# Unit 0's second token group with seven block products, unit 1's v in unit 0's buffer, and the sums of w2 behind the conversions

## The chip, the cores and the metric

One core of one Trainium2 chip runs the program. The metric is the device time of one execution in microseconds (us); the kernel before takes 663.11 us, the median of three runs that lie between 662.74 and 663.75. The engines have these names in the profile: PE is TensorE (matrix products), PEld its weight loads, DVE is VectorE, ACT is ScalarE, POOL is GpSimd and SP is SyncE. DMA queues are fed from POOL, SP and ACT.

## The reference

A gated linear recurrence with complex decay runs over 768 steps for 4 x 8 heads of width 48; its outputs, laid out as 3072 tokens of 384 numbers, go through a two-layer network with a squared relu.

```python
mag = np.sqrt(a_re * a_re + a_im * a_im)
scale = np.minimum(mag, 0.999) / (mag + 1e-06)
a_re_n, a_im_n = (a_re * scale, a_im * scale)
for t in range(S):
    new_re = ar * S_re - ai * S_im
    new_im = ar * S_im + ai * S_re
    S_re, S_im = (new_re + kv, new_im)              # kv: outer product of k and v at t
    y[:, :, t] = np.einsum('bhd,bhde->bhe', q[:, :, t], S_re)
h = x @ w_in                                         # x: y as (3072, 384); w_in (384, 2048)
r = np.maximum(h, 0.0)
out = (r * r) @ w_out                                # w_out (2048, 384)
```

## The kernel before

The 3072 tokens are taken in six **units** of 512. For each unit the program does two kinds of work.

The **chain** of a unit runs mostly on DVE and ACT. It normalises the decays (L982 to L1006), multiplies them up within groups of four steps (`inner`, L1026 and L1034), turns the group products to the other layout on PE (L1060), scans them (L1107 to L1188), turns them back (L1060 again), and then, in `apply`, forms the scaled keys and queries: four products (L1261), two sums (L1278, into `aq`), squares on ACT (L1292), their sum (L1299), a logarithm and an exponential on ACT (L1301, L1306), and the keys and queries (L1309 to L1326, into `f`). The table `HOMES` may put the two sums (and the sum of squares) of one `apply` on PE, as products with the identity into a PSUM bank (L1267, L1268); the squares are then two ACT operations (L1286), and later steps read the bank.

The **pairs** of a unit (four, of two heads each) are the attention proper: keys and queries are transposed, either on PE (`turn_pe`, L1440, copied out by ACT at L1444; the table `BY_PE` names these pairs) or by DVE's transpose and DMAs (`turn`, L1414, L1419); scores on PE (L1461), masked by DVE into `A` (L1464); products of keys and v for the carried state (L1489, summed by DVE at L1503); outputs (L1520 and L1524, the "mix"), copied by ACT (L1533) and put into `xT` by DMA. Scores and mixes use parts of the PE array, all other products the whole array.

The **two-layer network** of a unit comes in two token groups of 256. The first layer is L1571 (96 matmuls for a unit, squared relu on ACT at L1604 and L1605). The second layer is either `dense` (32 matmuls with 384 columns for a group, L1619, copied by ACT at L1624) or `seven` (the groups in the table `SEVEN`, and both of the last unit): seven block products instead of eight, as 56 matmuls with 192 columns (L1682), with eight DVE sums of the hidden values (`put`, L1698), and DVE sums of the results (L1707) in place of ACT copies. `seven` needs four sums of blocks of w2, made once by `sums_of_w2` as eight DVE operations (L1672) into the tile `T`.

The weights arrive as 8-byte floats in 16 pieces, eight of w_in and eight of w_out, and are **converted** by ACT (L859) and DVE (L866, then L870, then L873). Pieces with an index of at least `SOON` use a second ACT operation (L864) in place of L870.

L1380 are products with the identity whose results nobody reads; the planner puts them into PE's gaps of the first 60 us.

The rows of a profile name a matmul of 4-byte numbers twice (its two passes): 32 matmuls L1619 are 64 records. Transposes on PE are recorded once.

The order on each engine is not written by hand. Every step is given to a planner (`Plan`) with an engine, an assumed duration, what it reads and writes, and a rank; `Plan.order` fills a modelled schedule greedily by rank, and the program is emitted in that order. `LANES`, `LANDED`, `SETTLED`, `GROUP`, `MLAT` and such are numbers of that model: for instance, after the modelled time `SETTLED` PE puts scores and mixes next to each other where it can. `ROOM` is the number of units that have a v buffer (and spare buffers inside `T`) of their own: with `ROOM = 2` unit 1 keeps its v, a third `QT` and a third `A` in the tile `T`, and the sums of w2, which need that space, come after unit 1's pairs.

Of the kernel before, what the change touches and what calls it, by code (L numbers as in the profile page):

```python
# [481 lines left out]
class Plan:  # L482
# [3 lines left out]
    MARGIN = 0.3  # L486
    SLACK = 1.7
    RATE = 280e3
    LANES, LANDED = 8, 0.2
    STOP, COLD = 2.4, 3.5  # L490
    TURN = 0.12
    SETTLED, GROUP = 90.0, 6
    HOLD, URGENT, FILL = {"DVE": 0.15, "ACT": 0.8}, (2, 0.2), (2, 0.2)
    DRAIN = {"DVE": 0.12, "ACT": 0.13}

# [127 lines left out]
def fast_path(ctx, tc, q, k, v, a_re, a_im, moe_w_in, moe_w_out, out, flag):  # L623
# [10 lines left out]
    NP = H // 2  # L634
# [13 lines left out]
    Y = HH * W * D  # L648
    EARLY = 2
    FINE = [(0, 0), (0, 1), (1, 0), (1, 1), (2, 0), (2, 1)]  # L650
    SOON = 4
    LEAD = 2
    LATER = 6
    HOMES = {(0, 0, 0): ("sc0", "sc1", None), (0, 0, 1): ("yp", "tr1", "tr0")}
    FILLS = 16, 12, 8
    LOADS = 1.0, 4.0
    NEAR, GLAT, TLAT, MLAT = 7.5, 2.0, 1.0, 1.0
    BY_PE = [(0, i) for i in range(NP)] + [(1, i) for i in range(3)]
    ROOM = 2
    SEVEN = [(1, 0), (1, 1), (2, 0), (2, 1), (3, 0), (3, 1), (4, 0), (4, 1), (5, 0), (5, 1)]  # L660

    dve, pool, act, sp = nc.vector, nc.gpsimd, nc.scalar, nc.sync
    pe = nc.tensor
# [89 lines left out]
    def vs(n):  # L753
        return n % 2 if n < ROOM else 0

    def tt(n):
        return n / 960.0 + 0.07
# [34 lines left out]
    CHAIN, PAIR, DENSE, CONV, LATE = 2, 1, 3, 3, 5  # L792
# [54 lines left out]
    def convert(i):  # L847
        held = tuple(plan.wrote[("a", 1)][1]) if SOON <= i < NPIECE else ()
        _, t, keys, dst, n, wk = piece(i)
# [4 lines left out]
        def part(dtype, i):  # L854
# [5 lines left out]
             after=later)  # L860
        mixed = SOON <= i < 2 * NPIECE
        if mixed:
# [90 lines left out]
    def chain(n):  # L953
# [284 lines left out]
        def apply(z, p, np):  # L1238
# [12 lines left out]
            rk = late[z]  # L1251
            home = HOMES.get((n, z, p), (None, None, None))
            held = [[(b,)] if b else [] for b in home]
# [117 lines left out]
    def take(kind, n):  # L1371
        s = slot[kind]
        slot[kind] = s + 1
        return s % n
# [9 lines left out]
    def pairs(n, which):  # L1384
# [9 lines left out]
        def turn(i):  # L1394
            z = i // 2
            s = take("QT", 3 if 0 < n < ROOM else 2)
            t = QT[s].rearrange("p (i x) -> p i x", i=W)
# [26 lines left out]
        def turn_pe(i):  # L1424
            z = i // 2
            s = take("QT", 3 if 0 < n < ROOM else 2)
            got["T", i] = s
# [20 lines left out]
        def score(i, h):  # L1448
# [3 lines left out]
            sa = bank[b].rearrange("p (j t) -> p j t", j=W)  # L1452
            a = take("A", 3 if 0 < n < ROOM else 2)
            got["A", i, h] = a
# [99 lines left out]
        for i in which:  # L1554
            (turn_pe if (n, i) in BY_PE else turn)(i)
            for h in range(2):
# [6 lines left out]
    def dense(n, grp):  # L1563
# [11 lines left out]
        spare = ["sc0", "sc1", "yp"] if n < EARLY and grp == 0 else []  # L1575
        joint = (n, grp) in SEVEN
        fs = [(j, j + NT) if joint else (2 * j, 2 * j + 1) for j in range(NT)]
# [82 lines left out]
    def sums_of_w2():  # L1660
        for h in range(2):
            fl, fu = slice(4 * h, 4 * h + 4), slice(NT + 4 * h, NT + 4 * h + 4)
            b00, b01 = w2[:, fl, 0:DH], w2[:, fl, DH:DM]
            b10, b11 = w2[:, fu, 0:DH], w2[:, fu, DH:DM]
            t3, t2, t4, s2 = (TW[r][:, fl] for r in range(4))
            lo, up = parts_of(h, 0), parts_of(h, 1)
            for o, x0, x1, reads, writes in (
                    (t3, b11, b01, lo + up, 0), (s2, b01, b00, lo, 3),
                    (t2, b11, s2, up + [("T", 3, h)], 1), (t4, b10, t2, up + [("T", 1, h)], 2)):
                writes = [("T", writes, h), ("t", writes)] + (tkeys[writes] if writes < 3 else [])  # L1670
                step("DVE", tt(4 * DH), reads, writes, lambda o=o, x0=x0, x1=x1:
                     dve.tensor_tensor(out=o, in0=x0, in1=x1, op=ALU.subtract),  # L1672
                     (PAIR, 1.5))

    def gk(x, r, h):
        return [("gh"[x], HW * h + i, r) for i in range(HW)]
# [219 lines left out]
    for n in range(NU):  # L1896
        load(n)
        if n == 0:
            for i in range(NPIECE):
                fetch(i)  # L1900
            for i in range(SOON):
                convert(i)
        rest = chain(n)
        if n == 0:
            for j in (0, 1, 2):
                fetch(NPIECE + j)
        if n == 0:
            fill(FILLS[2], [("lv", 0)], lv[:, 0])
            for z in range(2):
                rest(z)  # L1910
                pairs(n, (2 * z, 2 * z + 1))
            for i in range(SOON, NPIECE):
                convert(i)
        else:
            rest(0, 1)
            pairs(n, range(NP))
        if n == ROOM - 1:
            sums_of_w2()
        if n == 0:
            step("POOL", 0.2, xk(0, [NM - 1]), [("gate", 2)], lambda: pool.tensor_copy(  # L1920
                out=gate[:, 2:3], in_=xT[:, 0, NM - 1, L - 1:L]), (CONV, 0))
            for j in (3, 4):
                fetch(NPIECE + j, False)
            for j in range(NPIECE):
                convert(NPIECE + j)
                if j < 3:
                    fetch(NPIECE + 5 + j, False)
        if n == NU - 1:
            eleven(n)
        for grp in range(2):  # L1930
            (seven if n == NU - 1 else dense)(n, grp)
    for i in range(2 * NPIECE):
# [58 lines left out]
```

## Time and profile before

| what | value |
| --- | --- |
| median of three runs | 663.11 us (662.74 to 663.75) |
| the profiled execution | 663.12 us |
| its span, first to last instruction | 661.2 us |
| PE busy | 620.8 us, 94% |
| DVE busy | 583.9 us, 88% |
| ACT busy | 347.0 us, 52% |
| mean granted TensorE clock | 0.99 |
| start of the first long run of first-layer products (L1571), unit 0 | 83.44 us |
| start of the same for unit 1, 2, 3, 4 | 191.19, 288.35, 386.43, 483.24 us |
| start of the last unit's first layer (L1827) | 580.75 us |

The profiled execution is one of the runs that agree with the median within 0.01 us. Read it by stages: up to about 60 us PE has little to do and DVE is busy; from there PE works without a break to the end, unit by unit, some 97 us each, and fills the time in which the next unit's chain runs on DVE with the network of the unit before.

### The profile page before, as it was taken

What the parts mean: (1) busy time and instruction counts of PE and PEld (TensorE: products, weight loads), DVE (VectorE), ACT (ScalarE), POOL (GpSimd) and SP (SyncE); (2) the same over time, 40 slices, a digit from 0 to 9 for tenths busy, and PEclk for the clock granted to TensorE, in tenths of its full rate; (3) what the DMA queues carried; (4) which work ended last, traced back from release to release, by engine and by line L of the source; (5) the groups of instructions that cost most, each with busy time, mean ns of one, the idle gap of its engine ahead of it and who ended that gap; (6) DMA issues with size and microseconds to landing.
All of it is one profiled execution on the core that took longest, in us unless ns stands there. A gap on an engine that the chain in (4) does not pass through costs nothing.

```text
span 661.2 us, 12107 instructions
## 1 busy us (share of the span) xinstructions
PE 620.8 (94%) x4454; PEld 555.5 (84%) x4454; DVE 583.9 (88%) x1191; ACT 347.0 (52%) x606; POOL 118.7 (18%) x198
## 2 busy tenths in 40 slices
PE   0378999999999999999999999999999999999996
PEld 0357887687779988999989989989999989988996
DVE  7999999898998999998989888998879989559971
ACT  7748979985746345348263357363366352045300
POOL 7401040401100032040121040111040111032200
PEclk9979999999999999999999999999999999999999
DMA  7953686305530055570056571046470054367730
GB/s 227 313 224 79 150 208 187 70 3 153 143 89 1 7 133 143 134 185 1 12 128 165 133 159 30 14 117 169 121 181 0 25 121 89 92 202 262 250 113 27
DMA packets 55268, 80.35 MB, mean 122 GB/s; under 512 B 11392, under 2 KB 37920, under 8 KB 55200
## 3 DMA queue, kind: packets, MB, share of 16 engines
q0 software_dynamic: 15424, 42.12, 22.5%
q1 hardware_dynamic: 35168, 31.93, 19.0%
q10 hardware_dynamic: 4608, 5.44, 3.2%
q8 instruction: 37, 0.61, 0.4%
q14 instruction: 31, 0.25, 0.1%
HBM read 48.76 MB, written 4.72 MB: 81 GB/s over the span
## 4 chain that ended last, share of the span: by engine, by line
PE 89%; DVE 7%; ACT 2%; issue 1%; DMA 1%; SPq 0%; DVEq 0%; ACTq 0%
PE d L1571 29%; PE d L1682 28%; PE d L1619 6%; PE sc L1461 5%; PE tr L1489 4%; PE yp L1520 3%; PE yp L1524 2%; PE d L1827 2%; PE tr L1827 2%; PE sc L1571 2%; PE sc L1827 1%; PE tr L1060 1%; DVE f L1261 1%; PE d L1440 1%; PE tr L1440 1%; PE yp L1571 1%
## 5 line engine op out<-in xcount | busy, mean ns | idle before, releaser
L1571 PE MATMUL d<-xT,w 128*128 128x256 f32 x888 | 198.5, 380 | 0.0
L1571 PEld LDWEIGHTS d<-xT,w 128*128 128x128 f32 x888 | 166.9, 190 | 23.1 <-issue 0.6
L1682 PE MATMUL d<-T,g 128*128 128x192 f32 x576 | 98.7, 327 | 0.0
L1682 PEld LDWEIGHTS d<-T,g 128*128 128x128 f32 x576 | 93.6, 190 | 0.3
L1604 ACT ACTIVATE g<-d 128x512 f32<-128x512 f32 x74 | 44.1, 596 | 83.6 <-PE d L1571 68.3
L1682 PE MATMUL d<-w,g 128*128 128x192 f32 x432 | 76.1, 329 | 0.0
L1637 POOL DMA_DIRECT2D out_dram<-ot x40 | 25.6, 644 | 277.6 <-DVE ot L1707 223.3
L1682 PEld LDWEIGHTS d<-w,g 128*128 128x128 f32 x432 | 70.4, 190 | 1.6 <-issue 0.7
L1362 POOL DMA_DIRECT2D KC<-f x60 | 32.4, 558 | 141.1 <-DVE f L1326 99.1
L1698 DVE TENSOR_TENSOR g<-g 128x512 f32<-128x512 f32 x72 | 48.5, 689 | 8.7 <-ACT g L1605 4.5
L1605 ACT ACTIVATE g<-g 128x512 f32<-128x512 f32 x80 | 50.5, 631 | 2.6
L1261 DVE TENSOR_TENSOR f<-aq,xn 128x384 f32<-128x384 f32 (+1 forms) x72 | 46.8, 687 | 0.0
L1619 PE MATMUL d<-w,g 128*128 128x384 f32 x128 | 44.0, 490 | 0.0
L1414 DVE STREAM_TRANSPOSE aq<-f 128x384 f32<-128x384 f32 (+1 forms) x51 | 42.7, 912 | 0.2
L1026 DVE TENSOR_TENSOR f<-aq 128x384 f32<-128x384 f32 x72 | 37.2, 554 | 0.8
L1461 PEld LDWEIGHTS sc<-QT 96*64 96x64 f32 x736 | 33.5, 137 | 3.6 <-issue 2.8
L1461 PE MATMUL sc<-QT 96*64 96x128 f32 (+1 forms) x736 | 36.0, 249 | 0.2 <-ACT QT L1444 0.2
L1619 PEld LDWEIGHTS d<-w,g 128*128 128x128 f32 x128 | 23.5, 190 | 13.7 <-issue 0.2
L1707 DVE TENSOR_TENSOR ot<-ot,d 128x192 f32<-128x192 f32 x70 | 23.7, 350 | 12.5 <-PE d L1682 12.0
L1464 DVE TENSOR_TENSOR A<-sc,mask 128x512 f32<-128x512 f32 x45 | 29.9, 685 | 3.2 <-PE sc L1461 3.1
L1533 ACT COPY yt<-yp 112x512 f32<-112x512 f32 (+1 forms) x20 | 11.6, 579 | 37.2 <-PE yp L1524 37.1
L1292 ACT ACTIVATE f<-aq 128x768 f32<-128x768 f32 (+1 forms) x16 | 17.3, 1082 | 24.7 <-DVE aq L1278 24.6
(279 smaller groups left out, 1119.5 us busy)
## 6 DMA issues: line engine op xcount, KB each, us to landing
QT<-aq SPq DMA_DIRECT2D x136, 64.0 KB, 2.0
f<-in_moe_w_in_dram POOLq DMA_DIRECT2D x8, 768.0 KB, 6.9
f<-in_moe_w_out_dram POOLq DMA_DIRECT2D x8, 768.0 KB, 5.1
QT<-aq ACTq DMA_DIRECT2D x68, 64.0 KB, 2.1
KC<-f POOLq DMA_DIRECT2D x40, 96.0 KB, 3.4
out_dram<-ot POOLq DMA_DIRECT2D x40, 96.0 KB, 3.7
xT<-yt SPq DMA_DIRECT2D x34, 96.0 KB, 2.4
T<-in_moe_w_out_dram POOLq DMA_DIRECT2D x4, 768.0 KB, 9.9
```

The source lines that it names most:

```text
L1026: lambda c=c, j=j: dve.tensor_tensor(out=f[:, j], in0=a[:, :, :, c - 1], in1=a[:, j, :, c].unsqueeze(1).to_broadcast([C, 2, HH, D]), op=AL ...
L1261: lambda j=j, r=r: dve.tensor_tensor(out=f4[:, j, r], in0=a[:, r], in1=over(j), op=ALU.mult), rk)
L1362: lambda i=i, p0=p0, m=m, src=src, queue=queue: queue.dma_start(out=kc[p0:p0 + m, i], in_=src),
L1414: lambda src=src, dst=dst: dve.transpose(out=dst, in_=src), rank)
L1461: pe.matmul(sa[p0:p0 + CH, j, t0:], lhsT=T[:, j, 1, h, t0:t0 + CH], rhs=T[:, j, 0, h, t0:], start=True, stop=True)
L1571: pe.matmul(ps, lhsT=w1[:, f // FP, m, ts(f % FP, C)], rhs=xT[:, n % 2, m, ts(grp, G)], start=(m == 0), stop=(m == NM - 1))
L1604: act.activation(out=o, in_=ps, func=AF.Relu)
L1605: act.activation(out=o, in_=o, func=AF.Square)
L1619: pe.matmul(ps, lhsT=gt[:, f % 2, ts(i, C)], rhs=w2[:, f], start=(f == 0), stop=(f == NF - 1))
L1682: pe.matmul(bank[b][:, 0:DH], lhsT=gsets[x][h][:, j - HW * h, r], rhs=w(j), start=first and j == 0, stop=last and j == NT - 1)
L1698: lambda: dve.tensor_tensor(out=g[:, :, o], in0=g[:, :, x0], in1=g[:, :, x1], op=op),
L1827: pe.matmul(ps[:, jj], lhsT=u[:, ts(jj, C)], rhs=v_, start=i == 0, stop=i == len(terms) - 1)
```

## The change

Tables and numbers of the planner change, one step's rank, and the place of one call.

```diff
-    LANES, LANDED = 8, 0.2
+    LANES, LANDED = 7, 0.2
-    SETTLED, GROUP = 90.0, 6
+    SETTLED, GROUP = 200.0, 6
...
-    SOON = 4
+    SOON = 3
-    HOMES = {(0, 0, 0): ("sc0", "sc1", None), (0, 0, 1): ("yp", "tr1", "tr0")}
+    HOMES = {(0, 0, 1): (None, None, "tr0")}
-    NEAR, GLAT, TLAT, MLAT = 7.5, 2.0, 1.0, 1.0
-    BY_PE = [(0, i) for i in range(NP)] + [(1, i) for i in range(3)]
-    ROOM = 2
-    SEVEN = [(1, 0), (1, 1), (2, 0), (2, 1), (3, 0), (3, 1), (4, 0), (4, 1), (5, 0), (5, 1)]
+    NEAR, GLAT, TLAT, MLAT = 7.5, 2.0, 1.0, 1.2
+    BY_PE = [(0, i) for i in range(NP)] + [(1, i) for i in range(4)]
+    ROOM = 1
+    SEVEN = [(0, 1), (1, 0), (1, 1), (2, 0), (2, 1), (3, 0), (3, 1), (4, 0), (4, 1), (5, 0), (5, 1)]
...
                 step("DVE", tt(4 * DH), reads, writes, lambda o=o, x0=x0, x1=x1:
                      dve.tensor_tensor(out=o, in0=x0, in1=x1, op=ALU.subtract),
-                     (PAIR, 1.5))
+                     (CHAIN, 1.05))
...
             pairs(n, range(NP))
-        if n == ROOM - 1:
-            sums_of_w2()
         if n == 0:
...
         if n == NU - 1:
             eleven(n)
+        if n == ROOM - 1:
+            sums_of_w2()
```

Counted over the whole program, the order has on PE 32 matmuls L1619 fewer (64 to 32), 56 matmuls L1682 more (560 to 616), 16 transposes L1440 more (112 to 128), and 4 each of L1267 and L1268 fewer (5 to 1 each). On DVE there are 4 more L1278 (32 to 36), 8 more L1698 (80 to 88), 7 more L1707 (70 to 77), 3 fewer L1414 (51 to 48) and 1 fewer L870 (4 to 3). On ACT there is one more L864 and 4 more L1444, two fewer L1624 and one more L1702, and four L1286 have become two more L1292. Unit 1's pairs now change on PE between parts of the array and the whole array 24 times, before 16 times.

The first place is DVE at the end of unit 0's pairs. `A` and `St` belong to the last pair from the second mask row on; `w_66` is w_in under conversion; L982 is the first step of unit 1's chain. Before:

```order
L870 SCALAR_TENSOR_TENSOR w_66<-g,w_66 128x768
L873 ISA w_66<-g,w_66 128x1536
L866 TENSOR_SCALAR w_66<-w_67 128x768
L870 SCALAR_TENSOR_TENSOR w_66<-w_67,w_66 128x768
L1464 TENSOR_TENSOR A_87<-sc_114,mask 128x512
L1464 TENSOR_TENSOR A_88<-sc_115,mask 128x512
L982 TENSOR_TENSOR f_70<-f_70 128x768
L1503 TENSOR_TENSOR St_90<-tr_117,St_90 96x96 x2
```

With the change:

```order
L982 TENSOR_TENSOR f_70<-f_70 128x768
L1503 TENSOR_TENSOR St_89<-tr_116,St_89 96x96 x2
L873 ISA w_66<-g,w_66 128x1536
L1503 TENSOR_TENSOR S_86<-tr_117,St_89 96x96
L866 TENSOR_SCALAR w_66<-g 128x768
L870 SCALAR_TENSOR_TENSOR w_66<-g,w_66 128x768
L873 ISA w_66<-g,w_66 128x1536
L1464 TENSOR_TENSOR A_87<-sc_114,mask 128x512
L1464 TENSOR_TENSOR A_88<-sc_115,mask 128x512
L866 TENSOR_SCALAR w_66<-w_67 128x768
L1503 TENSOR_TENSOR St_90<-tr_117,St_90 96x96 x2
```

L982 has moved ahead of the last pair's masks; one L870 is gone, and the L866 that stood before it has moved behind the masks.

The second place is DVE where unit 1's scan begins (L1087 and L1107, which read the turned products); `w_67` is w2, and `T` and `T_73` its sums. Before:

```order
L866 TENSOR_SCALAR w_67<-T 128x768
L1026 TENSOR_TENSOR f_71<-aq_69 128x384
L1034 TENSOR_TENSOR xn<-f_71 128x192 x2
L873 ISA w_67<-T,w_67 128x1536
L1087 COPY e<-ce 128x3
L1089 MEMSET e 128x3
L1087 COPY e<-ce 128x3
L1089 MEMSET e 128x3
L1107 TENSOR_TENSOR KC_76<-e 128x384
```

With the change:

```order
L1672 TENSOR_TENSOR T<-w_67 128x768
L873 ISA w_67<-T,w_67 128x1536
L1034 TENSOR_TENSOR xn<-f_71 128x192 x2
L1672 TENSOR_TENSOR T<-w_67,T_73 128x768
L1672 TENSOR_TENSOR T<-w_67 128x768
L1672 TENSOR_TENSOR T<-w_67,T 128x768
L1087 COPY e<-ce 128x3
L1089 MEMSET e 128x3
L1087 COPY e<-ce 128x3
L1089 MEMSET e 128x3
L1672 TENSOR_TENSOR T<-w_67,T_73 128x768
L1107 TENSOR_TENSOR KC_76<-e 128x384
```

Four of the sums of w2 stand in the L1672 rows before L1087, a fifth just before and a sixth just after L1107; before, one of these six stood in unit 1's pairs and five behind them. The other two (`T_73`) stand among the conversions in both.

The third place is PE at unit 1's scan; L1060 turns the scanned products (`xn`) back, between products of unit 0's first layer (L1571) for the second token group. Before:

```order
L1619 MATMUL d_112<-w_67,g 128x384 x4
L1571 MATMUL d_111<-xT,w_66 128x256 x6
L1571 MATMUL d_112<-xT,w_66 128x256 x6
L1571 MATMUL d_113<-xT,w_66 128x256 x3
L1060 MATMUL tr_116<-ident,xn 128x128 x3
L1571 MATMUL d_113<-xT,w_66 128x256 x3
L1060 MATMUL tr_117<-ident,xn 128x128 x3
L1571 MATMUL d_111<-xT,w_66 128x256 x6
L1571 MATMUL d_112<-xT,w_66 128x256 x6
L1571 MATMUL d_113<-xT,w_66 128x256 x6
L1571 MATMUL d_111<-xT,w_66 128x256 x6
L1619 MATMUL d_112<-w_67,g 128x384 x4
```

With the change:

```order
L1619 MATMUL d_112<-w_67,g 128x384 x4
L1571 MATMUL d_113<-xT,w_66 128x256 x3
L1571 MATMUL d_111<-xT,w_66 128x256 x6
L1571 MATMUL d_112<-xT,w_66 128x256 x6
L1571 MATMUL d_113<-xT,w_66 128x256 x6
L1571 MATMUL d_111<-xT,w_66 128x256 x3
L1060 MATMUL tr_116<-ident,xn 128x128 x3
L1060 MATMUL tr_117<-ident,xn 128x128 x3
L1571 MATMUL d_111<-xT,w_66 128x256 x3
L1571 MATMUL d_112<-xT,w_66 128x256 x6
L1571 MATMUL d_113<-xT,w_66 128x256 x6
L1571 MATMUL d_111<-xT,w_66 128x256 x6
L1682 MATMUL d_112<-w_67,g 128x192 x4
```

Before, 15 of the L1571 shown stand ahead of the first L1060 `ident` and three between the two; with the change 24 stand ahead of the first and none between, and behind them come L1682 in place of L1619. Counted from the program's start, 69 L1571 stand ahead of the first before and 75 with the change, and 32 L1619 in both.

## The prediction, made before the change was run

> **What bounds the kernel now.** I read the engines' totals and the chain of waits first, then windows by stage, then PE's waits.
>
> ```profile
> PE 620.8 (94%) x4454; PEld 555.5 (84%) x4454; DVE 583.9 (88%) x1191; ACT 347.0 (52%) x606; POOL 118.7 (18%) x198
> PE 89%; DVE 7%; ACT 2%; issue 1%; DMA 1%; SPq 0%; DVEq 0%; ACTq 0%
> ```
>
> PE has the largest total and 89% of the chain. But the totals mix stages, so the windows come next (span, then busy time of PE, PEld, DVE, ACT, POOL, granted clock, DMA share, GB/s):
>
> ```profile
> 30.00:40.00 10.00, 3.15 (x15) 3.18 (x16) 9.06 (x36) 6.34 (x11) 2.90 (x4) 0.51 1.02 318
> 60.00:83.00 23.00, 22.54 (x304) 20.11 (x304) 22.31 (x47) 20.28 (x32) 3.01 (x6) 1.00 0.63 147
> 83.00:151.00 68.00, 67.78 (x292) 52.10 (x289) 65.61 (x141) 57.67 (x95) 16.68 (x24) 1.00 0.45 118
> 151.00:191.00 40.00, 40.00 (x388) 30.75 (x386) 36.91 (x68) 24.74 (x48) 5.95 (x10) 1.00 0.52 143
> ```
>
> Up to 60 us DVE is full and PE mostly waits. From 60 to 151 both are full: PE 22.54 of 23 and 67.78 of 68, DVE 22.31 and 65.61. After 151 PE has no gap, while DVE has 3 us in 40. The waits of PE (total, times, longest) say where DVE holds it:
>
> ```profile
> PE d L1380 <- DVE yt L1119: 8.4, 1, 8.4
> PE d L1440 <- DVE f L1326: 2.3, 2, 1.6
> PE tr L1060 <- DVE xn L1188: 0.7, 2, 0.5
> PE tr L1520 <- DVE St L1503: 0.5, 1, 0.5
> ```
>
> Three places count for this change: the first keys of unit 0 (L1440 on L1326), the last sum of its pairs (L1520 on L1503), and the scan of unit 1, where PE waits for L1188:
>
> ```profile
> 134.14 0.55 PE L1060 MATMUL tr<-ident,xn 128*128 128x128 f32 x3 [0.22 <-DVE xn L1188]
> ```
>
> There DVE arrives 0.22 us after PE, so any work that DVE gains before this point arrives at PE almost undiminished. Everything behind it is PE work without a gap. So the end moves by how much later PE gets past unit 1's scan, plus the change of PE work behind it, plus new waits. Units 2 to 5 keep their order but for a few runs of products that are split otherwise.
>
> **Term 1: DVE's work up to unit 1's scan.** What matters on DVE is how its queue is composed between the end of unit 0's scan and L1188.
>
> ```profile
> 49.30 1.02 DVE L1278 TENSOR_TENSOR aq<-f 128x384 f32<-128x384 f32 x2
> 78.30 0.55 DVE L866 TENSOR_SCALAR w<-w 128x768 uint32<-128x768 uint32 x1
> 78.89 0.96 DVE L870 SCALAR_TENSOR_TENSOR w<-w,w 128x768 uint32<-128x768 uint32 x1
> 79.77 1.28 DVE L1464 TENSOR_TENSOR A<-sc,mask 128x512 f32<-128x512 f32 x2
> 80.97 0.95 DVE L982 TENSOR_TENSOR f<-f 128x768 f32<-128x768 f32 x1
> 81.83 0.53 DVE L1503 TENSOR_TENSOR St<-tr,St 96x96 f32<-96x96 f32 x2
> ```
>
> Rows overlap slightly; from start to start an L1278 takes 0.47 (two in 0.94), L870 0.88 (78.89 to 79.77) and L982 0.86 (80.97 to 81.83). Four L1278 come back from PE: +1.88. One conversion loses its L870: -0.88. L982 and the L866 pass the masks in opposite directions and are ahead of the last sum of the state in both orders: 0. So that sum comes 1.0 us later. The sums moved into the scan weigh more:
>
> ```profile
> 118.75 0.96 DVE L873 CUSTOM_DVE_ANT_0 w<-T,w 128x1536 uint16<-128x1536 uint16 x1 [0.17 <-ACT T L864]
> 121.68 0.96 DVE L873 CUSTOM_DVE_ANT_0 w<-T,w 128x1536 uint16<-128x1536 uint16 x1 [0.37 <-ACT T L864]
> 123.22 0.60 DVE L1087 COPY e<-ce 128x3 f32<-128x3 f32 x1 [0.27 <-ACT e L1075]
> 133.27 1.49 DVE L1188 TENSOR_TENSOR xn<-KC 128x384 f32<-128x384 f32 x2
> 193.54 2.88 DVE L1672 TENSOR_TENSOR T<-w,T 128x768 f32<-128x768 f32 x3
> ```
>
> Three L1672 take 2.88, about 0.9 each from start to start; six of the eight now stand ahead of the first L1188 instead of in or behind unit 1's pairs: +5.3. They fill DVE's waits for ACT, 0.17, 0.37 and 0.27: -0.8. L1188 thus comes 1.0 + 5.3 - 0.8 = 5.5 us later. The order of PE gives part of this back: 75 L1571 stand ahead of the first L1060 `ident` in place of 69, and 21 instead of 24 stand behind the second. Their price:
>
> ```profile
> 88.02 5.18 PE d L1571 x24
> 136.15 10.53 PE L1571 MATMUL d<-xT,w 128*128 128x256 f32 x48
> ```
>
> A matmul is two records, so 0.216 x 2 = 0.43 us. The second L1060 needs the second of the two L1188, which ends at 133.27 + 1.49 = 134.76 before and 5.5 later, at 140.3, now. PE then needs 0.4 for its three transposes, so it goes on at 140.7, against 136.15 before: +4.5. Three matmuls fewer are left behind it: -1.3. That makes +3.2; I take **+3.0**, as the added work may use small gaps of DVE. Does PE really get there too early? It is itself delayed by the last sum (1.0), by two L1571 that it did ahead of that sum and now does behind it (four records, 0.86), and by the six extra ones (12 records, 2.6):
>
> ```profile
> 79.64 1.10 PE L1571 MATMUL d<-xT,w 128*128 128x256 f32 x4
> ```
>
> That is 4.5 against DVE's 5.5, so PE waits about 1 more than the 0.22. The bounds: if L1188 does not hold PE, only its own 1.3 to 1.9 is left (1.3 where the L866 that now stands behind the masks takes less than the L982 that stood there); if DVE's waits for ACT stay, +3.8 to +4.0.
>
> **Term 2: PE's work behind it.** The second group of unit 0 swaps 32 L1619 (64 records) for 56 L1682 (112 records); 16 L1440 are added, as unit 1's last pair is turned on PE.
>
> ```profile
> 103.56 5.16 PE d L1619 x16
> 211.97 5.20 PE d L1682 x32
> 73.88 1.77 PE d L1440 x16
> ```
>
> 64 x 5.16/16 = 20.6 goes; 112 x 5.20/32 = 18.2 and 16 x 1.77/16 = 1.8 come: **-0.7**. So the eighth of the second layer that is saved, 2.4 us, is mostly spent on the turned pair. The three L1414 that the pair needed are gone from DVE, 2.4 us by the row below, in a stretch where PE sets the pace: 0.
>
> ```profile
> 169.34 2.47 DVE L1414 STREAM_TRANSPOSE aq<-f 128x768 f32<-128x768 f32 x3
> ```
>
> **Term 3: alternations.** In unit 1's pairs PE switches between a part of the array and the whole of it 24 times, before 16.
>
> ```profile
> 157.17 1.49 PE sc L1461 x32
> 167.02 0.82 PE sc L1461 x16
> 167.84 1.49 PE d L1619 x4
> 173.11 1.29 PE d L1619 x4
> ```
>
> Two score runs apart cost 2 x 0.82, together 1.49: 0.15. Four L1619 records take 1.49 right behind scores and 1.29 behind whole-array work: 0.20. Not every alternation shows as much in the rows of its neighbours, so I take 0.1 each; eight more make **+0.8**; bounds 0 and +1.6.
>
> **What costs nothing.** Eight L1698 and seven L1707 are new on DVE in unit 1's pairs:
>
> ```profile
> L1698 DVE TENSOR_TENSOR g<-g 128x512 f32<-128x512 f32 x72 | 48.5, 689 | 8.7 <-ACT g L1605 4.5
> L1707 DVE TENSOR_TENSOR ot<-ot,d 128x192 f32<-128x192 f32 x70 | 23.7, 350 | 12.5 <-PE d L1682 12.0
> ```
>
> 8 x 0.6 and 7 x 0.3 (start to start) are 6.9 us, against the 5.3 of L1672 and 2.4 of L1414 that leave the same stretch or the one behind it. PE covers them as long as its mix finds the masks; by my sum of the rows the first mix of unit 1 arrives within 0.5 us of its masks, so this cover is thin. I take 0 and keep +2 as its price. Two more edits stand here:
>
> ```profile
> 42.80 0.91 PE L1267 MATMUL sc<-f,ident 128*128 128x384 f32 x2
> 89.13 4.63 POOL L949 DMA_DIRECT2D v<-in_v_dram  x6
> QT<-in_moe_w_out_dram POOLq DMA_DIRECT2D x2, 768.0 KB, 9.7
> 98.88 1.05 DVE L866 TENSOR_SCALAR w<-QT 128x768 uint32<-128x768 uint32 x2
> ```
>
> On PE 16 records L1267 and L1268 vanish, at some 0.4 each 6 us, between the first at 42.80 and the keys at 53.77, where PE waits for DVE anyway: 0. Unit 1's v, now in unit 0's buffer, waits for unit 0's last mix, and its six loads (4.63) stand on POOL ahead of the two fetches of w2 into `QT`, which stood ahead of them before. With 9.7 to landing the pieces come at about 103 instead of 98; DVE reads them at 98.88 before, and about 104 with the change, as its order has put the conversions of `QT` behind others: 0, and up to +1 on DVE if they come late.
>
> **The sum**: 663.12 (the profiled execution; the median is 663.11) + 3.0 - 0.7 + 0.8 = **666.2 us**, slower.
>
> **The rivals.** *Faster* (661.3): PE sets the pace from 60 on, not DVE. For it: PE's 22.54 of 23. The first keys come earlier, since on DVE three sums and products fewer stand ahead of
>
> ```profile
> 52.70 1.01 DVE L1326 TENSOR_TENSOR f<-f,sc 128x384 f32<-128x384 f32 x2
> 53.77 2.13 PE L1440 MATMUL d<-ident,f 128*96 128x128 f32 x16 [1.64 <-DVE f L1326]
> ```
>
> and one L866 more, 3 x 0.47 - 0.5 = 0.9. If that gain went through and the sums of w2 found enough gaps on DVE (2.4 us from 83 to 151), the end would be -0.9 - 0.7 - 0.2. Against it: L1520 waited 0.46 for the last sum, and DVE gains 5.5. It decides if the first L1060 `ident` of unit 1 waits for nothing and L1571's first long run starts before 83. *No change* (663.7): L1188 comes late, but PE's own delay is +1.3 and hides it, alternations free: +1.3 - 0.7. *Cold clock* (667.3): with the products of HOMES gone, PE has between 43 and 52 little but eight L1380 and one pair of L1267 and L1268. After the wait of 8.4 the granted clock was 0.51 in the window from 30 to 40. At half clock the 2.13 of the first L1440 would be 4.3, and half of that would pass to DVE's first masks: +1.1. The Trainium skill (TensorE: Matmul & The Clock Gate, section "Part 1: The HAM clock gate (the "warmup" mystery)") has the clock halve after an idle window of about 3.4 us; by this rule the longest new gap, some 3 us by the sum of DVE's rows from the pair of products to the first keys, is just short of it, and the forecast would stand. *Starved mix* (668.2): the first mix of unit 1 waits for masks that stand behind six L1698 on DVE, +2; for it the thin cover, against it that only one pair is so close.
>
> **Chances.** Forecast 0.43, faster 0.17, no change 0.15, cold clock 0.12, starved mix 0.13. A measurement tells this kernel from no change by 0.2%, 1.3 us: below 661.8 faster, above 664.4 slower. Faster 0.17, same 0.15, slower 0.68. The forecast's own range, from the bounds of its terms, is 664.6 to 667.6; 8 in 10 need part of both sides: 661.6 to 668.5.
>
> **What would show it.** Right: the last L1503 of unit 0 about 1 us later; L1188 near 138.8; PE waiting about 1 us for it; the second layer of unit 0 with its last L1682 before unit 1's first layer, and every later unit shifted by the same 3 us. Wrong: no wait at L1188; or shifts that grow from unit to unit; or a clock under 0.9 between 48 and 60.

## The result, and the profile after

| | before | changed kernel |
| --- | --- | --- |
| median, first comparison (4 runs each) | 663.43 us | 667.65 us, ratio 1.0059 [1.0041, 1.0077] |
| median, second comparison (15 and 10 runs) | 663.87 us | 667.77 us, ratio 1.0051 [1.0035, 1.0068] |
| span of the profiled execution | 661.2 us | 667.9 us (666.7 in the second comparison) |

The changed kernel is slower by 4.2 and 3.9 us, against +3.1 forecast and inside the range. Its first profiled execution, 669.64 us, is 2 us above its median, so every reading below is also held against a second profile of it (668.53 us).

The page of the changed kernel, engine totals and shares of the chain of waits:

```profile
PE 621.0 (93%) x4502; PEld 563.1 (84%) x4502; DVE 588.5 (88%) x1206; ACT 350.6 (52%) x608; POOL 119.6 (18%) x198
PE 82%; DMA 8%; DVE 5%; ACT 2%; issue 1%; SPq 0%; POOL 0%; ACTq 0%; DVEq 0%
```

PE's busy time is the same as before, 621.0 us against 620.8, so the longer span is time in which PE has nothing to do. DMA has gone from 1% of the chain to 8%. Much of that is the loads at the start of the program, but transfers into `xT` are among it now. PE's waits in the changed kernel (total, times, longest):

```profile
PE tr L1267 <- ACT f L1292: 2.1, 1, 2.1
PE d L1571 <- DMA xT<-yt: 2.0, 2, 1.3
...
PE yp L1520 <- DVE A L1464: 0.9, 1, 0.9
PE d L1440 <- DVE f L1326: 0.8, 2, 0.5
PE d L1682 <- DVE ot L1707: 0.7, 1, 0.7
```

Behind 60 us three of these are new and longer than half a microsecond: 2.0 us for `xT`, the input of the first layer; 0.9 us for masks in unit 0's pairs, which all kernels of the changed order have; and 0.7 us near the end, which the second profile lacks. The wait that the forecast was built on, L1060 on L1188, is missing from the list. PE's timeline shows the places:

```profile
69.56 0.53 PE L1520 MATMUL yp<-A,v 128*48 128x128 f32 x5 [0.95 <-DVE A L1464]
...
85.57 0.70 PE L1571 MATMUL d<-xT,w 128*128 128x256 f32 x2
...
90.09 1.97 PE L1571 MATMUL d<-xT,w 128*128 128x256 f32 x8 [0.67 <-DMA xT<-yt]
...
140.38 0.83 PE L1060 MATMUL tr<-ident,xn 128*128 128x128 f32 x6
...
201.08 2.18 PE L1571 MATMUL d<-xT,w 128*128 128x256 f32 x9 [1.33 <-DMA xT<-yt]
```

DVE's timeline of the same kernel, the end of unit 0's pairs and unit 1's scan:

```profile
84.60 0.25 DVE L1503 TENSOR_TENSOR S<-tr,St 96x96 f32<-96x96 f32 x1
...
139.13 1.48 DVE L1188 TENSOR_TENSOR xn<-KC 128x384 f32<-128x384 f32 x2
```

L1188 starts at 139.13, where 138.8 was forecast. PE's L1060 at 140.38 nevertheless stands without a wait: PE came no earlier. The second profile has the same (138.97 and 140.22); its one wait for L1188, 0.4, stands in unit 0.

Where the time goes can be read from one table of start times (us); the last two columns are experiments explained below:

| place | before | changed | changed, 2nd profile | late v | late v, short sums |
| --- | --- | --- | --- | --- | --- |
| last L1524 of unit 0's pairs ends | 83.51 | 85.64 | 85.58 | 83.95 | 83.99 |
| first L1060 `perm` of unit 1 | 121.47 | 125.50 | 125.33 | 122.96 | 123.00 |
| L1188 of unit 1 (DVE) | 133.27 | 139.13 | 138.97 | 136.56 | 134.76 |
| first L1060 `ident` of unit 1 | 134.14 | 140.38 | 140.22 | 137.85 | 137.89 |
| first L1060 of unit 2 | 200.79 | 206.34 | 206.00 | 202.24 | 202.26 |
| first L1060 of unit 3 | 297.26 | 302.81 | 302.47 | 298.71 | 298.74 |
| first L1060 of unit 4 | 396.62 | 402.29 | 401.83 | 398.10 | 398.11 |

From unit 2 to unit 4 the shift stands still, as forecast (+5.55, +5.55, +5.67 for the changed kernel's first profile): it has arisen by 206 us. The span grows by 6.7; the rest of that lies near the end, 0.7 of it in the wait named above. GpSimd's timeline in the changed kernel shows what is new beside the first wait for `xT`:

```profile
84.83 4.51 POOL L949 DMA_DIRECT2D v<-in_v_dram  x6 [8.14 <-ACT f L991]
91.20 1.48 POOL L1918 COPY gate<-xT 128x1 f32<-128x1 f32 x1 [1.86 <-DMA xT<-yt]
92.63 1.44 POOL L844 DMA_DIRECT2D QT<-in_moe_w_out_dram  x2
```

Unit 1's loads of v are issued at 84.83, while the last transfers into `xT` are under way. In the kernel before, the six loads at 89.13, behind these transfers, are unit 2's, and unit 1's go into `T` much later (ns of one issue, then the first and the last start):

```profile
L949 POOL DMA_DIRECT2D T<-in_v_dram x6: 683/690/899, 122.9 to 126.8; - x6
```

The list of DMA issues from 83 to 92 us (KB each, median us from issue to landing) prices this, first for the kernel before:

```profile
xT<-yt SPq DMA_DIRECT2D x2, 48.0 KB, 2.5
xT<-yt ACTq DMA_DIRECT2D x2, 48.0 KB, 2.7
```

and for the changed kernel:

```profile
v<-in_v_dram POOLq DMA_DIRECT2D x2, 192.0 KB, 5.2
v<-in_v_dram POOLq DMA_DIRECT2D x4, 96.0 KB, 5.6
xT<-yt SPq DMA_DIRECT2D x2, 48.0 KB, 4.4
xT<-yt ACTq DMA_DIRECT2D x2, 48.0 KB, 4.9
```

The same four transfers take about 2 us longer to land. With one buffer of v for all units, unit 2's loads now wait for unit 1's last mix (they stand at 194.93), and so fall beside the transfers of unit 1's last pair; that is the second wait, 1.33.

### The profile page after: what moved, and what is told of

The parts are those of the page before. It is cut to its first block, busy times and chain, and to the rows that moved or that the text cites. A ratio compares the mean times of both kernels' runs of the same rounds, so it can differ in the third digit from the quotient of the medians.

```text
span 667.9 us, 12201 instructions
## 1 busy us (share of the span) xinstructions
PE 621.0 (93%) x4502; PEld 563.1 (84%) x4502; DVE 588.5 (88%) x1206; ACT 350.6 (52%) x608; POOL 119.6 (18%) x198
## 4 chain that ended last, share of the span: by engine, by line
PE 82%; DMA 8%; DVE 5%; ACT 2%; issue 1%; SPq 0%; POOL 0%; ACTq 0%; DVEq 0%
PE d L1571 28%; PE d L1682 28%; PE sc L1461 4%; PE tr L1489 3%; PE d L1619 3%; PE yp L1520 3%; PE yp L1524 2%; DMA w<-in_moe_w_in_dram 2%; PE d L1827 2%; DMA xT<-yt 2%; PE sc L1827 1%; PE tr L1060 1%; PE sc L1571 1%; PE tr L1827 1%; PE tr L1440 1%; DMA aq<-in_a_im_dram 1%
## 5 line engine op out<-in xcount | busy, mean ns | idle before, releaser
L1571 PE MATMUL d<-xT,w 128*128 128x256 f32 x888 | 198.7, 381 | 2.0 <-DMA xT<-yt 2.0
L1571 PEld LDWEIGHTS d<-xT,w 128*128 128x128 f32 x888 | 166.8, 190 | 26.0 <-issue 3.6
L1682 PE MATMUL d<-T,g 128*128 128x192 f32 x640 | 110.5, 328 | 0.0
L1682 PEld LDWEIGHTS d<-T,g 128*128 128x128 f32 x640 | 103.8, 190 | 0.8 <-issue 0.2
L1682 PE MATMUL d<-w,g 128*128 128x192 f32 x480 | 84.5, 328 | 0.0
L1682 PEld LDWEIGHTS d<-w,g 128*128 128x128 f32 x480 | 78.3, 190 | 1.4 <-issue 0.6
L1698 DVE TENSOR_TENSOR g<-g 128x512 f32<-128x512 f32 x80 | 53.7, 690 | 4.8 <-ACT g L1605 2.8
L1414 DVE STREAM_TRANSPOSE aq<-f 128x384 f32<-128x384 f32 (+1 forms) x48 | 40.3, 914 | 0.2
L1707 DVE TENSOR_TENSOR ot<-ot,d 128x192 f32<-128x192 f32 x77 | 26.0, 350 | 16.2 <-PE d L1682 15.5
L1461 PE MATMUL sc<-QT 96*64 96x128 f32 (+1 forms) x768 | 38.2, 250 | 0.2 <-ACT QT L1444 0.2
L1461 PEld LDWEIGHTS sc<-QT 96*64 96x64 f32 x768 | 35.1, 137 | 3.8 <-issue 2.4
L1520 PE MATMUL yp<-A,v 128*48 128x128 f32 x376 | 35.2, 277 | 0.9 <-DVE A L1464 0.9
L1464 DVE TENSOR_TENSOR A<-sc,mask 128x512 f32<-128x512 f32 x48 | 31.9, 685 | 3.7 <-PE sc L1461 3.6
L1292 ACT ACTIVATE f<-aq 128x768 f32<-128x768 f32 (+1 forms) x18 | 19.0, 1055 | 27.1 <-DVE aq L1278 27.0
L1489 PEld LDWEIGHTS tr<-v,KC 128*96 128x96 f32 x320 | 30.2, 165 | 1.8 <-issue 0.7
L1489 PE MATMUL tr<-v,KC 128*96 128x48 f32 x320 | 31.0, 247 | 0.1
```

What stands on the lines that cost most here:

```text
L1414: lambda src=src, dst=dst: dve.transpose(out=dst, in_=src), rank)
L1461: pe.matmul(sa[p0:p0 + CH, j, t0:], lhsT=T[:, j, 1, h, t0:t0 + CH], rhs=T[:, j, 0, h, t0:], start=True, stop=True)
L1489: pe.matmul(ps[:, j, h], lhsT=kc[:, j, (2 * i + h) % HH], rhs=v5[:, j, 2 * i + h], start=True, stop=True)
L1520: pe.matmul(ps[64 * h:64 * h + D, j - js[0]], lhsT=v5[:, j, 2 * i + h], rhs=aa[h][:, j], start=True, stop=at[j] is None)
L1571: pe.matmul(ps, lhsT=w1[:, f // FP, m, ts(f % FP, C)], rhs=xT[:, n % 2, m, ts(grp, G)], start=(m == 0), stop=(m == NM - 1))
L1682: pe.matmul(bank[b][:, 0:DH], lhsT=gsets[x][h][:, j - HW * h, r], rhs=w(j), start=first and j == 0, stop=last and j == NT - 1)
```

## The experiments

In the kernels from the third group on, the planner's order of the changed kernel is kept and single steps are moved in it: `out` is the list of steps in that order, `at` a step's place in it, `tags` holds the steps of a kind, and `move(a, b)` puts the steps `a` right behind `b`. Their line numbers are 7 to 20 higher than those of the kernel before; the matching line is named where a row is shown. The letters of the theories belong to each expectation alone.

**The changed kernel again.**

> The changed kernel again, for a second profile of it. Theory A (the loss is made ahead of 86 us: PE colder and DVE longer ahead of unit 0's pairs): 667.5, the first long run of L1571 about 1 us later than before (near 84.5 to 85.5), the granted clock again near 0.55 from 48 to 56. Theory B (the loss is made at unit 1's scan, as the prediction has it): 667.5, L1188 near 139 and PE waiting for it. Theory C (the first profile had an unlucky start of its loads): the wait for xT at 199 and the wait of 0.74 for L1707 at 644 are gone, and the span is near 665.8.

Measured: 667.77 us, ratio 1.0051 [1.0035, 1.0068]; `xT` waits of 1.6 in its profile, in the same two places. The wait near the end is gone, and PE waits for no L1188 of unit 1. The granted clock was 1.00 from 48 to 52 us and 0.54 from 52 to 56; the transposes of the first keys (L1440 at 53.63) took 3.65 us, 2.13 before the change, and DVE waited for the scores behind them:

```profile
58.81 0.69 DVE L1464 TENSOR_TENSOR A<-sc,mask 128x512 f32<-128x512 f32 x1 [0.78 <-PE sc L1461]
```

**One table entry undone, everything planned anew.** Three kernels each put one line of the change back:

```diff
-    SOON = 3
+    SOON = 4
```

> SOON back to 4, the rest as changed. If the ACT operation L864 that comes ahead of unit 0's scan copies (L1145) costs time, 0.5 to 1 us less than the changed kernel, 666.5 to 667, with unit 0's second L1188 that much earlier. If it is hidden, 667.5; DVE then has 0.9 more ahead of unit 0's last masks, and the first long run of L1571 is up to 0.5 later.

Measured: 671.98 us, ratio 1.0109 [1.0081, 1.0137].

```diff
-    HOMES = {(0, 0, 1): (None, None, "tr0")}
+    HOMES = {(0, 0, 0): ("sc0", "sc1", None), (0, 0, 1): ("yp", "tr1", "tr0")}
```

> The sums of the first two applies back on PE, the rest as changed. Theory A: the clock from 48 to 56 is 1.0 again, the first keys and the first long run of L1571 are 1 to 2 us earlier than in the changed kernel, and the end is at 665.5 to 666. Theory B: PE waits longer for L1188, and the end stays within 0.5 of 667.5, less 1.0 at most for the four sums that leave DVE.

Measured: 707.39 us, ratio 1.0628 [1.0593, 1.0662].

```diff
-    SEVEN = [(0, 1), (1, 0), (1, 1), (2, 0), (2, 1), (3, 0), (3, 1), (4, 0), (4, 1), (5, 0), (5, 1)]
+    SEVEN = [(1, 0), (1, 1), (2, 0), (2, 1), (3, 0), (3, 1), (4, 0), (4, 1), (5, 0), (5, 1)]
```

> Unit 0's second group in dense form again, the rest as changed; the sums of w2 keep their early place. By the prediction's second and third term PE has 2.4 us more work in this group, fewer changes of array part (0 to 0.8 less), and DVE 6.9 less in unit 1's pairs: 669 to 670 if PE alone sets the pace there, 667 to 668 if the eight sums of the hidden values and the thin cover of the masks cost about 2 us.

Measured: 693.69 us, ratio 1.0458 [1.0429, 1.0487].

All three are slower than the changed kernel itself, one by 40 us. PE's waits in the second of them say why:

```profile
PE d L1571 <- DMA xT<-yt: 12.5, 6, 3.3
...
PE yp L1520 <- DVE A L1464: 4.8, 5, 1.9
PE sc L1461 <- DVE A L1464: 3.4, 1, 3.4
```

Nearly all of these are waits behind 290 us, in units that the undone line does not touch: the planner's numbers fit together, and one of them put back gives another order of the whole program. Nothing about a single part follows from these three, except one reading of the second up to 84 us: there the granted clock was 1.00 from 48 to 56 us and unit 0's first layer began at 83.41, as before the change. From here on the order is held fixed.

**The loads of v, both held back.** Unit 1's go behind the fetches of w2 into `QT`, where unit 2's stood before the change, and unit 2's behind the last pair of unit 1, behind a copy that waits for that pair's `xT`:

```diff
+        v1, v2 = (sorted(tags[("v", n)], key=at.get) for n in (1, 2))
+        move(v1, max(tags[("fetch", NPIECE + 3)] + tags[("fetch", NPIECE + 4)], key=at.get))
+        move(v2, max(tags[("xT", 1)], key=at.get))
+        out.insert(out.index(v2[0]), lambda: pool.tensor_copy(
+            out=gate[:, 2:3], in_=xT[:, 1, NM - 1, L - 1:L]))
```

> Every engine keeps the order of the changed kernel, but POOL issues unit 1's loads of v behind the gate that waits for unit 0's last xT (and behind the two fetches into QT), and unit 2's loads behind a new gate of the same kind for unit 1. Theory C (the loads of v share the DMA engines with the last pair's xT and make it late): PE's waits for xT, 0.5 at 90 and 1.1 at 200, are gone, 1.4 to 1.8 us less than the changed kernel, 666.0 to 666.4. If xT is late for another reason, the waits stay, and so does the time.

Measured: 665.22 us, ratio 1.0017 [1.0005, 1.0029], about 2.5 us less than the changed kernel and more than the 1.4 to 1.8 expected. The DMA issues of this kernel from 83 to 92 us:

```profile
xT<-yt SPq DMA_DIRECT2D x2, 48.0 KB, 1.9
xT<-yt ACTq DMA_DIRECT2D x2, 48.0 KB, 2.2
```

PE's waits for `xT` are gone, and so is the one near the end. The busy time from 83 to 203 us (span, then PE, PEld, DVE, ACT, POOL, clock, DMA share, GB/s) in the changed kernel, second profile:

```profile
83.00:203.00 120.00, 118.36 (x805) 99.39 (x804) 116.31 (x239) 86.14 (x147) 23.76 (x34) 1.00 0.44 115
```

and with the late loads:

```profile
83.00:203.00 120.00, 120.00 (x803) 101.49 (x802) 115.10 (x237) 87.27 (x148) 23.41 (x35) 1.00 0.42 111
```

PE's 1.64 us without work have gone. From the last L1524 of unit 0 to the first L1060 of unit 2 PE takes 118.29 us here, against 120.70 and 120.42 in the two profiles of the changed kernel: 2.1 to 2.4 less. By the medians 1.1 us are still lost against the kernel before. In this profile it is 1.45 at unit 2: 0.44 up to the end of unit 0's pairs, the rest in a stretch in which PE has no gap at all.

**The loads of unit 2 alone held back** (the edit above without the line that moves `v1`).

> The changed kernel with only unit 2's loads of v held back behind the last pair of unit 1; unit 1's stay beside the transfers of unit 0's last pair. If the loads delay the transfers into xT where they stand beside them: the wait of TensorE for xT near 200 us (1.1 to 1.3) is gone and the one near 90 us (0.5 to 0.7) is there, and the time is 1.1 to 1.5 us below the changed kernel (667.7): 666.2 to 666.6. If only the two together, or something else in the kernel with the late loads, made the difference: no more than 0.5 us below, 667.2 or more; or all 2.5 us, 665.2.

Measured: 665.91 us, ratio 1.0031 [1.0020, 1.0043]: by the ratios 1.3 us less than the changed kernel (1.0051) and 0.9 more than with both held back (1.0017). The wait near 200 us is gone, the first one is there with 0.5. So unit 2's loads cost about 1.3, and 0.9 is left for unit 1's, which were not held back alone.

**The six sums of w2 behind the scan.** They move right behind the second L1188 of unit 1:

```diff
+        late = [n for k, n in enumerate(tags["sums"]) if k % 4 != 1]
+        move(sorted(late, key=at.get), max(tags[("xn", 1)], key=at.get))
```

> The order of the changed kernel, but the six sums of w2 into T stand on DVE right behind unit 1's two L1188 instead of ahead of the scan. Theory B (DVE is the one that is late at unit 1's scan): L1188 comes 5.3 earlier, PE's second L1060 1 us or more earlier, and the end with it, 666.5 or less. Theory A (PE itself is as late there as DVE): PE passes the scan at the same time as in the changed kernel within 0.4, and the end is unchanged, 667.3 to 667.8.

Measured: 671.49 us, ratio 1.0113 [1.0093, 1.0132], slower than with the sums ahead. L1188 came at 136.06, only some 3 us earlier than in the changed kernel; part of that is an earlier end of unit 0's pairs, and DVE waited 2.1 for ACT in the scan, which it does not with the sums there. Behind L1188 the six stand in the way of unit 1's keys, and PE waited 1.7 for those and 2.5 for `xT`. So the place ahead of the scan was the better of the two. It does not say what the sums cost there.

**The six sums cut short.** With the late loads of v, each of the six forms 16 of its 768 columns:

```diff
-                step("DVE", tt(4 * DH), reads, writes, lambda o=o, x0=x0, x1=x1:
+                few = slice(0, DH if len(tags["sums"]) % 4 == 2 else 4)
+                step("DVE", tt(4 * DH), reads, writes, lambda o=o[:, :, few], x0=x0[:, :, few], x1=x1[:, :, few]:
                      dve.tensor_tensor(out=o, in0=x0, in1=x1, op=ALU.subtract),
```

> The kernel with the late loads of v (665.2); the six L1672 that stand ahead of unit 1's scan form 16 of 768 columns each (the rest of their results is left out), every order as it was. Theory A (term 1 of the prediction: through L1188 these sums make TensorE late by most of their 5.3 us less 0.8): L1188 comes 3 to 4.5 us earlier (132.0 to 133.5), and TensorE's first ident transposes of unit 1 and the end by 2 to 3 us: 662.2 to 663.2. Theory B (TensorE has no gap from unit 0's last mix on, and reaches these transposes 0.7 us behind L1188 by its own work): L1188 comes earlier just as much, and the time stays at 665.2 within 0.5, as does the stretch from the last L1524 of unit 0 to the first L1060 of unit 2.

Measured: 664.92 us, ratio 1.0013 [1.0004, 1.0022], beside 1.0017 with the sums whole. PE's timeline with whole sums (L1068 is the kernel's L1060, L1580 its L1571):

```profile
133.75 4.26 PE L1580 MATMUL d<-xT,w 128*128 128x256 f32 x19
137.85 0.82 PE L1068 MATMUL tr<-ident,xn 128*128 128x128 f32 x6
138.50 3.83 PE L1580 MATMUL d<-xT,w 128*128 128x256 f32 x17
```

and with short ones:

```profile
133.79 4.26 PE L1582 MATMUL d<-xT,w 128*128 128x256 f32 x19
137.89 0.82 PE L1068 MATMUL tr<-ident,xn 128*128 128x128 f32 x6
138.54 3.83 PE L1582 MATMUL d<-xT,w 128*128 128x256 f32 x17
```

PE does the same at the same times, so with the late loads the sums ahead of the scan cost nothing; in the changed kernel itself PE waits for unit 1's L1188 in neither profile. L1188 itself came 1.8 us earlier, less than the 5 us of work removed, and DVE's timeline in that kernel says why (L880 is L873, L1095 is L1087, L1083 is ACT's copy L1075 of the turned products):

```profile
121.30 0.97 DVE L880 CUSTOM_DVE_ANT_0 w<-T,w 128x1536 uint16<-128x1536 uint16 x1 [0.76 <-ACT T L871]
...
124.59 0.17 DVE L1095 COPY e<-ce 128x3 f32<-128x3 f32 x1 [1.50 <-ACT e L1083]
```

DVE waits for a conversion of ACT's, reaches the scan early all the same, and then waits for the `perm` transposes, which PE does at 123.0 in its own order. From these to L1188 it takes 11.76 us with short sums, 13.60 with whole ones, 11.80 before the change.

**The six sums on GpSimd** (with the late loads of v, and behind the scan as in the edit above):

```diff
+                eng = dve if len(tags["sums"]) % 4 == 2 else pool
-                step("DVE", tt(4 * DH), reads, writes, lambda o=o, x0=x0, x1=x1:
-                     dve.tensor_tensor(out=o, in0=x0, in1=x1, op=ALU.subtract),
+                step("DVE", tt(4 * DH), reads, writes, lambda o=o, x0=x0, x1=x1, eng=eng:
+                     eng.tensor_tensor(out=o, in0=x0, in1=x1, op=ALU.subtract),
```

> The kernel with the late loads of v (665.2), and six of the eight sums of w2 on GpSimd instead of VectorE, behind the output transfers of unit 0, so that VectorE reaches L1188 without them. Theory A (term 1 of the prediction: the six sums make TensorE late): L1188 of unit 1 comes some 4.5 to 5 us earlier, and some 2 to 3 us of that arrive at the end: 662.2 to 663.2. Theory B (TensorE has no gap from unit 0's last mix to the second transposes of unit 2, and is as late by its own work): L1188 comes earlier, but the time stays at 665.2 within 0.6. Theory C (GpSimd and VectorE slow each other): VectorE's rows beside the sums grow by 10% or more, and the time is 666 or more.

Measured: 675.86 us, ratio 1.0183 [1.0164, 1.0203], 10.6 us more than with the sums on DVE. GpSimd's timeline:

```profile
129.76 1.82 POOL L1685 TENSOR_TENSOR T<-w 128x768 f32<-128x768 f32 x1
131.53 1.81 POOL L1685 TENSOR_TENSOR T<-w,T 128x768 f32<-128x768 f32 x1
133.31 1.80 POOL L1685 TENSOR_TENSOR T<-w 128x768 f32<-128x768 f32 x1
135.07 5.45 POOL L1685 TENSOR_TENSOR T<-w,T 128x768 f32<-128x768 f32 x3
```

and DVE's (L1115 is L1107):

```profile
128.53 0.25 DVE L1115 TENSOR_TENSOR KC<-e 128x96 f32<-128x96 f32 x1
...
129.12 9.63 DVE L1115 TENSOR_TENSOR KC<-yt,e 128x96 f32<-128x96 f32 x1
138.79 1.86 DVE L1127 TENSOR_TENSOR yt<-KC 128x24 f32<-128x24 f32 x2
```

An operation that takes some 0.26 us on DVE lasted 9.63, and the two after it ended when GpSimd's last sum did. DVE stood still for nearly all of the sums' 10.8 us. L1188 came at 145.53, 9.0 later than with the sums on DVE, and PE waited 8.3 for it. That gives the slack that DVE had there: some 0.6 us (8.97 less 8.35).

**More products in the gap of the first keys**, to keep the clock up, in the changed kernel:

```diff
+        k = out.index(max(tags["fill"], key=at.get)) + 1
+        out[k:k] = [lambda: pe.matmul(bank["d2"][:, 0:C], lhsT=ident, rhs=ident,
+                                      start=True, stop=True)] * 8
```

> The order of the changed kernel with eight more products that nobody reads on PE behind the fill of 47 us. The granted clock from 48 to 56 rises from 0.55-0.77 to near 1. If the cold clock costs time (the rival of the prediction), first masks 0.5 to 1 us earlier and the end at 666.6 to 667.1; if DVE's queue hides it, masks within 0.2 and the end at 667.4 to 667.8.

Measured: 669.38 us, ratio 1.0071 [1.0054, 1.0088]. Windows of the changed kernel (granted clock after the five busy times):

```profile
48.00:52.00 4.00, 1.88 (x12) 1.58 (x10) 4.00 (x11) 2.83 (x6) 0.00 (x0) 0.55 0.00 0
52.00:56.00 4.00, 3.97 (x14) 2.54 (x15) 3.97 (x11) 3.97 (x5) 1.12 (x2) 0.59 0.05 9
```

and with the added products:

```profile
48.00:52.00 4.00, 4.00 (x26) 3.13 (x24) 4.00 (x12) 3.85 (x7) 0.00 (x0) 0.92 0.00 0
52.00:56.00 4.00, 2.68 (x26) 2.00 (x26) 3.97 (x9) 3.97 (x8) 1.12 (x2) 1.00 0.41 86
```

The clock is up and no time is won. From the first key (L1326) to the first mask (L1464) it takes 5.40 us here, as in the first profile of the changed kernel, and 5.54 with the late loads, whose clock is 0.58 from 52 to 56; but 6.26 in the second profile of the changed kernel, where DVE waited for the scores. So the cold clock costs between nothing and 0.9 there, and it differs from execution to execution. By the ratios the kernel became slower by 1.3 us, with intervals that overlap: its profile has waits of 2.5 for `xT`, and one of 1.1 for a DMA into `KC` at 77.55 that the changed kernel lacks. Why was not followed further.

**The four sums of `apply` as products on PE again**, order fixed.

```diff
-    HOMES = {(0, 0, 1): (None, None, "tr0")}
+    HOMES = {(0, 0, 0): ("sc0", "sc1", None), (0, 0, 1): ("yp", "tr1", "tr0")}
```

> The order of the changed kernel, but the four sums of the first two applies are PE products in banks again, as before the change, so DVE has four L1278 fewer ahead of unit 0's pairs. By the prediction's first term this gives back the 1.9 us of DVE: last sum of unit 0's pairs and first long run of L1571 1.5 to 2 us earlier than in the changed kernel. If unit 1's scan then waits for DVE (3.4 of the 5.3 of the sums left uncovered), the end gains 1.0 to 1.9: 665.7 to 666.6; if the four sums were hidden, less than 0.3.

Measured: 671.22 us, ratio 1.0103 [1.0082, 1.0123]. From 40 to 60 us DVE now waits for ACT (L1323 is L1309, L1320 is L1306):

```profile
DVE f L1323 <- ACT f L1320: 3.1, 1, 3.1
```

The squares fall to other operations of ACT, which take places in the fixed order that were not chosen for them. This says nothing about the price of the sums.

**Fewer alternations in unit 1's pairs**, with the late loads of v: each pair's second run of scores moves up behind its first (`place` is a step's position in the fixed order).

```diff
+        for i in range(NP):
+            a, b = sorted(tags[("sc", 1, i)], key=place.__getitem__)
+            place[b] = place[a] + 0.001
```

> The kernel with the late loads of v (665.2), and in each of unit 1's four pairs the second run of scores moved up to stand right behind the first, so that TensorE alternates eight times less there; no engine's order changes otherwise. Term 3 of the prediction (0.1 us for each alternation where TensorE has no gap): -0.8, 664.4, bounds 663.6 to 665.2; the two runs of scores together take 1.49 instead of 1.64 or more, and the stretch from unit 1's L1188 to the first products of its first layer is shorter by 0.6 to 0.8. Rival: the later products for the state or a later wait take it back, TensorE waits in a mix: 665.2 or more.

Measured: 665.60 us, ratio 1.0026 [1.0013, 1.0038], no faster than 1.0017. PE's timeline (L1477 is L1461, L1505 is L1489, L1456 is L1440):

```profile
156.36 1.56 PE L1477 MATMUL sc<-QT 96*64 96x128 f32 x32
...
164.69 1.79 PE L1477 MATMUL sc<-QT 96*64 96x128 f32 x32
...
176.71 1.22 PE L1505 MATMUL tr<-v,KC 128*96 128x48 f32 x12
178.47 1.08 PE L1456 MATMUL tr<-ident,f 128*96 128x128 f32 x8 [0.55 <-ACT St L1515]
```

The first joined run takes 1.49 from start to start, and the stretch around it, from 155.82 to 158.66 without the joining, is 0.25 us shorter: about 0.12 for each of two alternations, as term 3 had it. But the second and third runs are longer, and in the third pair the products for the state come late and PE waits 0.55 for the copy that frees a bank. The price of an alternation shows in this one pair; taking it out by hand is paid with waits.

No kernel of these beats the one before.

## Why the prediction held, and where it did not

The forecast of 666.2 was right in sign and near in size, but of the two largest costs one was forecast and did not come, and the other came and was not in the forecast.

**Term 1, the last sum: +1.0.** In the two profiles of the changed kernel unit 0's pairs end 2.1 later than before, in the kernels with late loads 0.2 to 0.5, although up to 84 us all have the same order. The difference lies ahead of this term, which begins with the second L1188 of unit 0. That one starts at 41.56 before; at 43.26, 42.80 and 43.30 in the two profiles of the changed kernel and the one with unit 2's loads alone held back; and at 41.8 to 42.0 in the others whose order is the same up to there. The first three executions took 0.8 to 2.0 us more than the medians of their kernels, the others up to 0.8 less, so this is a spread of executions, and a profile's shift of 5.55 fits a median that is 4.2 later. From that L1188 to the end of the pairs it takes between nothing and 0.8 more than before (the kernel with the added products aside), so +1.0 was too large.

**Term 1, the two L1571 that now stand behind that sum: 0.86.** This held: from the end of unit 0's pairs to unit 1's `perm` transposes PE took 37.96 us before and 39.01 with the late loads, +1.05.

**Term 1, the sums of w2: this step failed.** "L1188 thus comes 1.0 + 5.3 - 0.8 = 5.5 us later" came true to 0.4 us, for another reason. The short sums move L1188 by 1.8, not by 5.3 - 0.8: without them DVE waits for ACT and PE. In the changed kernel the other 3.9 to 4.0 of L1188's delay come from PE, since the `perm` transposes, which the scan starts from, came that much later: 2.1 of it stands at the end of unit 0's pairs already, 1.05 is the term above, and the rest is the first wait for `xT`. The forecast took DVE as the one that holds PE; in fact PE made DVE late, and "PE waits about 1 more" did not happen. By the prediction's own test, no wait at L1188, this step is wrong. Its own lower bound, that only 1.3 to 1.9 is left if L1188 does not hold PE, is what the late loads show: 1.45 at the first L1060 of unit 2, with terms 2 and 3 in it.

**Terms 2 and 3: -0.7 and +0.8.** Before, PE's work from the end of unit 1's second `ident` transposes to the first long run of its first layer was 136.15 to 191.19, less four L1571 records done there early (0.86) and three matmuls that have moved ahead (1.3): 52.88. After, it is 141.05 to 194.31, 53.26. That is +0.4, against +0.1. The late loads have the same stretch, 138.50 to 191.77.

**"Unit 1's v [...] 0, and up to +1 on DVE": this step failed too.** The loads cost 2.3 to 2.8 us by the ratios (1.0051 to 1.0059 against 1.0017), and 2.1 to 2.4 of that show on PE between unit 0's last mix and unit 2. The prediction followed the queue on GpSimd, and what stood behind the loads there, the fetches into `QT`. It did not ask which transfers are in flight at the new time: the transfers into `xT`, for which PE waits next, land 2 us later beside the loads. It also took the loads at 89.13 for unit 1's. They are unit 2's, which the change of `ROOM` moves from there to 194.93, and for them it priced nothing.

So of the +3.1 of the sum only 1.1 came, by the medians (1.45 in the profile with late loads), and the missing 2.5 filled it up. That the sum came near the measured time is luck: a cost that did not come and one that was left out nearly cancelled. The rival *no change* had the right mechanism for the sums (PE's own delay hides L1188) and the wrong end, for it too lacked the loads. *Cold clock* happened, by the prediction's own sign of a clock under 0.9 between 48 and 60, and cost nothing in the first profile of the changed kernel, 0.1 with the late loads and 0.9 in the second profile of the changed kernel, near its price of 1.1; no run separates what the median has of it. The Trainium skill (TensorE: Matmul & The Clock Gate, section "Part 1: The HAM clock gate (the "warmup" mystery)") let one expect no halving here, its idle window being 3.4 us; the trace disagrees, see below. *Faster* had one part right: from the second L1188 of unit 0 to the first key it takes 9.7 to 10.3 us with the new order and 11.14 before. The gain was spent by the end of unit 0's pairs: from the first mask to there it takes 26.8 (27.7 with the added products), before 25.78, with PE's new wait for masks, 0.95, in between. *Starved mix* did not show: that wait is in unit 0, and PE has none for masks in unit 1.

## What to carry to other kernels

When a load is moved, list the transfers that will be in flight at its new time and ask which of them somebody waits for: its own queue is half of the answer. An engine that reaches a wait late is not shown to be held by it; look one step back for what both engines wait for, here the transposes that PE itself does late. Where a planner sets the order, hold the order fixed before undoing one part; three kernels planned anew told of the planner and not of the part.

## What the hardware showed

- Beside six loads of v (0.8 MB in all) four transfers of 48 KB landed after 4.4 to 4.9 us; with the loads held back they landed after 1.9 to 2.2, and before the change after 2.5 to 2.7.
- Beside six sums on GpSimd, each 1.8 us, a DVE operation with two inputs that takes 0.26 us lasted 9.63, to the end of the fifth sum. The Trainium skill (SBUF — State Buffer, section "Who interferes with whom") has the two engines share a pair of ports that one holds for a whole instruction while the other is blocked; the trace agrees that DVE was blocked, and adds that five instructions in a row passed before DVE got in. Why GpSimd came first it does not show: on record the DVE operation starts 0.64 us ahead of the first sum.
- In the first profile of the changed kernel the granted clock was 1.00 from 46 to 48 us, 0.60 from 48 to 50 and 0.50 from 50 to 54, though PE's longest gap from 40 to 50 us was 1.92; PE was busy 1.27, 0.81 and 1.88 of 2 us in the three windows from 44 to 50.
